# Retention and an ELU feed-forward on one core: two states moved to the end of the opening, four loads moved behind a transposition

## The chip, the cores and the metric

The kernel runs on one core of a Trainium2 chip. The metric is device microseconds of one execution. The engines go by the names of the profile: PE is TensorE, PEld its weight loads, DVE is VectorE, ACT is ScalarE, POOL is GpSimd, SP is SyncE, which only issues DMAs here.

## The reference

```python
scores = (1 / sqrt(64)) * q @ k.T                  # q, k, v: 8 batches, 8 heads, 576 rows, 64
D[h, i, j] = gamma[h] ** (i - j) if i >= j else 0  # gamma[h] = 1 - 2 ** (-5 - h)
x = (scores * D) @ v                               # heads side by side: 4608 x 512
h = x @ w_in                                       # 512 x 2048
g = where(h > 0, h, exp(min(h, 0)) - 1)
out = g @ w_out                                    # 2048 x 512, out 4608 x 512 float32
```

## The kernel before

**Retention.** The powers of gamma are split into a factor on the rows of q and one on the rows of k, so that a block of 128 rows needs its own masked scores and, for all that lies before it, one 64 x 64 state per head. A *unit* is one batch, one half of its first 512 rows (T is 0 or 1) and four of the eight heads; four units make a batch, numbered in order, so units 0 to 3 are batch 0 and unit 4 is the first of batch 1. The last 64 rows of four batches at a time make a *tail* (units 32 and 33). For a unit the kernel loads q, k and v (`ldq`, `ldk`, `ldv`, on SP), multiplies the four quarters of q and k by their factors (`cq0`, `cq1`, `ck0`, `ck1`, line 494), casts v (`cv`, line 545) and transposes q and k: units 0 to 6 on PE (`T`, line 558, copied out at line 564 by `cp`), unit 7 and all later ones with a DMA (`tr`, line 602). Units from number 8 on load q, k and v in two issues each (`ldq0_10`, `ldq1_10` and so on, line 412).

PE then computes scores (`sc`) and states; DVE masks the scores (`mask`, line 937); DVE, or ACT for the first, adds up the states (`mid`, `end`, lines 803 to 812). From the two sums come states with zeros beside the diagonal blocks, `bm` for the unit's own second half and `be` for whoever comes behind it (line 820, tile `s_end`; `bm` of units 0 and 1 is line 834). For a unit with T = 1, which is the case of units 2 and 3, nobody comes behind but the tail of the batch: `be2` and `be3` are read by unit 32 alone. The result goes through PSUM to `xt` (lines 972 to 993).

**Feed-forward.** Tokens are taken in blocks of 256 or 512. F1 multiplies `xt` by a column of w_in, ACT takes the exponential (`ex`, line 1145), ACT or DVE the maximum (`md`, lines 1153 and 1155), DVE joins them (`g`, line 1160), F2 multiplies g by w_out into the output. Weights come in eight pieces, `wi0` to `wi3` and `wo0` to `wo3`, issued by POOL (lines 471 and 479). F1 and F2 fill PE between the stretches of the units; a stretch (`S`) holds what the units before still need and the scores and states of the next.

**The order of the work.** Nothing of the order is written out by hand. Each step is an `Op` with a cost per engine that may do it, what it depends on, and a rank. `Plan.run` (line 68) goes through planned time and gives every free engine the ready step of the lowest rank (`pick`, line 99); a step with a choice of engines goes to the one that would end it first. The result is the order in which the instructions are issued, and each engine runs its own in that order. Three tables bear on the change: `ON` (line 212) binds a step to one engine, `RANKS` (line 202) adds to a rank, `HOLD` (line 201) makes POOL write one element into the tile of `ldq4` (`hold4`, line 431, rank -5), which keeps SP's loads from unit 4 on behind it. In a list `turn` stand steps that must have begun, not ended, before a step may. SP's loads form a chain by `turn`; a transposition has rank -1, loads have ranks from 9 up, so a transposition whose input is ready goes first.

```python
it.be = block(("end", n), ("s_end", it.b, it.T, it.w), f"be{n}", end)
return add(name, {"POOL": 0.62, "DVE": (0.42, 0.4 if it.early else 1.5)}, [dep], emit, it.rank + 3,
           take=[T(key[0], key, [P, 2, P], BF16)], use=[src])
...
held.append(add(f"hold{n}", {"POOL": 0.13}, [], emit_hold, -5, take=take))
...
it.turned.append(add(f"tr{n}", {"SP": 1.23}, list(it.cq.values()), emit, -1, ...
```

The ranks of units 2 and 3 are -56 and -52, so `be2` had rank -53 and `be3` -49; F1 and F2 start at rank 0. While the first 50 us of the plan have gaps on PE, small matmuls on zeros are put there.

Of the kernel before, what the change touches and what calls it, by code (L numbers as in the profile page):

```python
# [198 lines left out]

LEAD = 64  # L200
HOLD = {4: "wi0"}
RANKS = {}
TOGETHER = 1
EARLY = 5
LOOSE = True
# [3 lines left out]
POOL0 = 3.6  # L209
MERGE = {}  # L210
FROM = (8.96, 10.28, 13.13, 15.23, 17.0, 17.0, 17.44, 17.82)
ON = {'mid1': 'DVE', 'be2': 'DVE', 'md_1_0': 'ACT', 'xc1_2': 'DVE', 'cv0': 'DVE', 'md_1_1': 'ACT', 'cq12': 'DVE'}
DIRECT = True
PAIR = 8
FAR = 8
# [26 lines left out]
def kernel(  # L242
# [1069 lines left out]
    named = {op.name: op for op in plan.ops}  # L1312
# [6 lines left out]
    named["wo0"].turn.append(named["wi3"])  # L1319
    for name, e in ON.items():  # L1320
        if name in named and e in named[name].cost:
            named[name].cost = {e: named[name].cost[e]}
    for name, shift in RANKS.items():
        if name in named:
            named[name].rank += shift
# [64 lines left out]
```

## Time and profile before

| | |
|---|---|
| median of 3 runs | 298.99 us (298.35 to 299.23) |
| profiled execution | 299.29 us, span 297.6 us |
| PE busy | 291.7 us, 98% of the span, clock 1.00 |
| ACT, DVE, POOL busy | 66%, 60%, 46% |
| DMA queue of SP | 45.37 MB, 78.3% of 16 engines |
| DMA queue of POOL (weights) | 4.19 MB, 8.6% |
| chain that ended last | PE 86%, DMA 7%, POOL 3%, DVE 2% |

The span is what the profile covers from the first to the last instruction; the time of the execution is 1.69 us longer. Times in the text are microseconds from the span's start. A row of the timeline has its start, its length, the engine, the line and the operation, and behind them in brackets how long the engine stood idle before it and what ended that. A row of the chain of waits has start, length, and whose time it was; an engine's name with a q is its sequencer, which waits or issues.

### The profile page before, as it was taken

Reading aid. Unit: us, or ns where it says so; the run is one execution under the profiler, and the core shown is the slowest. Engines: PE = TensorE matmul, PEld = TensorE weight load, DVE = VectorE, ACT = ScalarE, POOL = GpSimd, SP = SyncE. Lnnn points to the kernel's source line nnn. Section 1 sums busy time; section 2 is a strip of 40 time slices with the busy share of each in tenths; the row PEclk is TensorE's granted clock in tenths of the full one; section 3 lists DMA queues with packets and bytes.
Section 4 is the critical chain, followed back from the end, with each engine's and each line's share of the span. In section 5 each row is a group of like instructions: output and inputs, shape, how many; then the busy total and the mean of one; then the engine's idle time right before and its main releaser. Section 6 shows DMA issues by size and latency. Waiting matters only on the chain.

```text
span 297.6 us, 8887 instructions
## 1 busy us (share of the span) xinstructions
PE 291.7 (98%) x3560; PEld 164.4 (55%) x3560; DVE 179.7 (60%) x323; ACT 195.1 (66%) x383; POOL 136.5 (46%) x257
## 2 busy tenths in 40 slices
PE   7999999999999999999999999999999999999996
PEld 3678746867776664545545454545444544444445
DVE  5999935838755849697756556666550169643300
ACT  2449823859768758778696868676772289777512
POOL 5880379956856755666534558542444000000000
PEclk9999999999999999999999999999999999999999
DMA  7999999999999999999999999996497410011132
GB/s 207 260 206 204 216 280 217 219 174 200 193 194 187 196 189 204 193 237 200 208 222 298 208 219 203 196 189 161 103 169 172 90 39 1 0 39 35 35 106 73
DMA packets 142010, 50.14 MB, mean 168 GB/s; under 512 B 120720, under 2 KB 137488, under 8 KB 141968
## 3 DMA queue, kind: packets, MB, share of 16 engines
q1 hardware_dynamic: 137744, 45.37, 78.3%
q0 software_dynamic: 4224, 4.19, 8.6%
q8 instruction: 28, 0.46, 0.7%
q14 instruction: 14, 0.11, 0.1%
HBM read 36.70 MB, written 9.44 MB: 155 GB/s over the span
## 4 chain that ended last, share of the span: by engine, by line
PE 86%; DMA 7%; POOL 3%; DVE 2%; SPq 1%; issue 0%; ACT 0%; ACTq 0%
PE f L276 84%; DMA rv<-in_v_dram 7%; PE sc L276 2%; POOL w_out_sb L479 1%; DVE pt L937 1%; SPq L422 1%; POOL w_in_sb L471 1%; POOL s_end L820 0%; POOL qkn L494 0%; DVE qkn L494 0%; PE f L558 0%; DVE s_end L820 0%; DVE s_mid L834 0%; POOL s_mid L820 0%; POOL vn L545 0%
## 5 line engine op out<-in xcount | busy, mean ns | idle before, releaser
L276 PE MATMUL f<-w_out_sb,g 128*128 128x512 bf16 (+2 forms) x608 | 141.1, 368 | 0.0
L276 PE MATMUL f<-xt,w_in_sb 128*128 128x256 bf16 (+1 forms) x768 | 138.2, 326 | 0.0
L1160 DVE SCALAR_TENSOR_TENSOR g<-e,f 128x512 bf16<-128x512 f32 x144 | 95.9, 684 | 69.0 <-ACT f L1153 53.2
L1145 ACT ACTIVATE e<-f 128x512 f32<-128x512 f32 x144 | 84.8, 597 | 33.7 <-PE f L276 25.7
L276 PEld LDWEIGHTS <-w_in_sb 128*128 128x128 bf16 x768 | 74.7, 98 | 53.5 <-DVE xt L988 0.4
L276 PEld LDWEIGHTS <-g 128*128 128x128 bf16 x608 | 56.6, 98 | 57.9
L1153 ACT ACTIVATE f<-f 128x512 f32<-128x512 f32 x116 | 68.5, 593 | 0.0
L494 POOL TENSOR_TENSOR qkn<-rqk,far_q 128x256 bf16<-128x256 f32 x48 | 28.9, 614 | 9.2 <-DMA rqk<-in_q_dram 9.0
L494 POOL TENSOR_TENSOR qkn<-rqk,far_k 128x256 bf16<-128x256 f32 x48 | 29.0, 616 | 7.6 <-DMA rqk<-in_k_dram 7.2
L1200 ACT COPY ot<-f 128x512 f32<-128x512 f32 (+2 forms) x30 | 16.8, 560 | 19.9 <-PE f L276 19.9
L545 POOL CAST vn<-rv 128x512 bf16<-128x512 f32 x28 | 17.1, 612 | 21.7 <-DMA rv<-in_v_dram 16.6
L972 ACT CAST xt<-f 128x512 bf16<-128x512 f32 x24 | 12.9, 589 | 16.1 <-PE f L276 16.1
L877 POOL CAST y<-mid 64x256 bf16<-64x256 f32 x36 | 14.3, 401 | 19.8 <-DVE mid L862 10.4
L1155 DVE TENSOR_SCALAR f<-f 128x512 f32<-128x512 f32 x28 | 19.4, 694 | 1.0 <-ACT e L1145 0.7
L931 DVE TENSOR_TENSOR pt<-sc,mask_t 128x1024 bf16<-128x1024 f32 x12 | 14.6, 1220 | 2.4 <-PE sc L276 2.4
L618 POOL TENSOR_TENSOR aside<-aside,gq 128x256 bf16<-128x256 f32 x16 | 9.4, 614 | 11.3 <-DMA aside<-in_k_dram 11.2
L494 POOL TENSOR_TENSOR qkn<-rqk,gq 128x256 bf16<-128x256 f32 x13 | 8.1, 633 | 12.3 <-DMA rqk<-in_q_dram 12.3
L877 ACT CAST y<-mid 64x256 bf16<-64x256 f32 x30 | 11.6, 402 | 2.1 <-DVE mid L860 1.0
L862 DVE TENSOR_TENSOR mid<-f,mid 128x256 f32<-128x256 f32 x24 | 10.2, 424 | 2.8 <-PE f L276 0.5
L276 PE MATMUL f<-pt,vn 64*64 64x64 bf16 (+1 forms) x512 | 11.5, 202 | 0.2 <-DVE pt L937 0.2
L993 ACT CAST xt<-f 128x256 bf16<-128x256 f32 x10 | 4.2, 452 | 10.8 <-PE f L276 10.8
L937 DVE TENSOR_TENSOR pt<-sc,mask 128x1024 bf16<-128x1024 f32 x8 | 9.8, 1220 | 2.2 <-PE sc L276 2.1
(92 smaller groups left out, 172.7 us busy)
## 6 DMA issues: line engine op xcount, KB each, us to landing
rqk<-in_q_dram SPq DMA_DIRECT2D x48, 128.0 KB, 3.9
rqk<-in_k_dram SPq DMA_DIRECT2D x48, 128.0 KB, 3.5
rv<-in_v_dram SPq DMA_DIRECT2D x48, 128.0 KB, 3.4
out_dram<-ot SPq DMA_DIRECT2D x18, 256.0 KB, 3.5
out_dram<-ot SPq DMA_DIRECT2D x19, 128.0 KB, 2.4
rqk<-in_q_dram SPq DMA_DIRECT2D x8, 256.0 KB, 6.8
rqk<-in_k_dram SPq DMA_DIRECT2D x8, 256.0 KB, 5.8
rv<-in_v_dram SPq DMA_DIRECT2D x8, 256.0 KB, 5.9
```

Of the source, the lines that this page charges most:

```text
L276: return pin(nc.tensor.matmul(*a, **kw))
L494: pin(alu[op.eng].tensor_tensor(dst, tiles[raw][:, :, e], g, ALU.mult))
L545: pin(copy[op.eng](tiles["vn", n], tiles["rv", n]))
L877: pin(copy[op.eng](dst, tiles[key][j * D : (j + 1) * D]))
L931: pin(nc.vector.tensor_tensor(tiles[it.pt].rearrange("p i h n -> p (i h n)")[:, : 2 * w * C].rearrange("p (i x n) -> p i x n", i=2, n=C), ...
L937: pin(nc.vector.tensor_tensor(tiles["pt", n].rearrange("p i h n -> p (i h) n"), tiles[it.sc].rearrange("p i (h n) -> p (i h) n", h=2), mas ...
L972: pin(copy[op.eng](by_block(it.xt)[:, 2 * it.T + c], tiles[xkey, c].rearrange("p (h n) -> p h n", n=P)))
L1145: pin(nc.scalar.activation(tiles[ekey], tiles[hkey], AF.Exp))
L1153: pin(nc.scalar.activation(ph, ph, AF.Relu))
L1155: pin(nc.vector.tensor_scalar_max(ph, ph, 0.0))
L1160: pin(nc.vector.scalar_tensor_tensor(tiles[gkey], tiles[ekey], -1.0, tiles[hkey], ALU.add, ALU.min))
L1200: pin(copy[op.eng](tiles[okey][:, :cols], tiles[pkey][:, :cols]))
```

## The change

`be2` is no longer bound to DVE, and the ranks of `be2` and `be3` rise by 60, to 7 and 11. `ldq0_10`, the first load of unit 10, may not begin before `tr7`, the DMA transposition of unit 7, has begun; by the chain, this holds for all later loads too.

```diff
-RANKS = {}
+AFTER = {"ldq0_10": "tr7"}
+RANKS = {"be2": 60, "be3": 60}
...
-ON = {'mid1': 'DVE', 'be2': 'DVE', 'md_1_0': 'ACT', 'xc1_2': 'DVE', 'cv0': 'DVE', 'md_1_1': 'ACT', 'cq12': 'DVE'}
+ON = {'mid1': 'DVE', 'md_1_0': 'ACT', 'xc1_2': 'DVE', 'cv0': 'DVE', 'md_1_1': 'ACT', 'cq12': 'DVE'}
...
+    for name, first in AFTER.items():
+        for one in (first if isinstance(first, tuple) else (first,)):
+            named[name].turn.append(named[one])
     for name, shift in RANKS.items():
         if name in named:
             named[name].rank += shift
```

## The prediction

> **What bounds the kernel now.** I read the page first: TensorE is busy for 291.7 us of a span of 297.6, no other engine above 66%, and the granted clock is full in every slice. So only TensorE's idle and waiting time can be won. The table by windows says where that is: 1.38 us idle before 5 us, 1.00 in 5 to 10, 0.27 and 0.11 in the next two, none from 20 to 35, 0.22 in 35 to 40, none again up to 100 us. The rest lies behind TensorE's last matmul (294.8 us). The list of TensorE's waits from 19 us to the end has one entry, 0.2 us, on a cast by POOL. The chain of waits tells what is behind that cast:
>
> ```profile
> 17.03 0.68 POOL qkn L494
> 17.71 3.00 POOL w_out_sb L479 x4
> 20.70 0.64 POOL s_end L820
> 21.35 0.05 POOL rqk L431
> 21.39 0.02 issue
> 21.41 0.37 SPq L422
> ...
> 22.37 15.56 DMA rv<-in_v_dram
> 37.94 0.05 issue
> 37.99 0.62 POOL vn L545
> ```
>
> The reader sees that POOL's block-diagonal state `be3` (0.64 us, line 820) stands directly ahead of the memset `hold4`, which lets SP ask for unit 4's q, k and v. They land at 30.64, 34.26 and 37.94, one every 3.65 us, because the weight pieces on the other DMA queue land between them (29.17, 32.79, 36.46, 40.15). TensorE's timeline shows what this costs:
>
> ```profile
> 35.26 0.60 PE L558 MATMUL f<-ident,qkn 128*128 128x128 bf16 x4
> 35.69 1.03 PE L276 MATMUL f<-w_out_sb,g 128*128 128x512 bf16 x4
> 36.65 0.42 PE L276 MATMUL sc<-qkT 64*64 64x128 bf16 x16
> 37.00 1.47 PE L276 MATMUL f<-w_out_sb,g 128*128 128x512 bf16 x6
> 38.65 0.32 PE L276 MATMUL f<-vn,qkn 64*64 64x64 bf16 x16 [0.18 <-POOL vn L545]
> ```
>
> Unit 4's key transposes take 0.43 us to the next row; the query ones, which waited for nothing, took 0.22 (31.99 to 32.22): 0.2 lost on k. The six matmuls from 37.00 last 1.65; six take 1.30 at 38.90, and each change to the small attention matmuls costs 0.09 anyway (the last one's step to them is 0.31 in 14 other places, not 0.22): 0.25 lost on v. Together **0.45 us** hangs on unit 4's loads.
>
> **The change, part by part.** I worked out the new order by hand from ranks and release rules; times are rows of the trace.
>
> *be3 behind hold4.* With rank 11 it loses to `hold4` (-5) when POOL is done with the weight issues at 20.70. The memset then starts 0.56 us sooner (21.25 to 20.69) and SP's first issue falls from 21.41 to 20.85. `be3` follows in a POOL idle until 30.77; only the tails (217 us) read it: cost nothing. Do the landings move as well? Unit 4's first packets show at 25.04, 3.6 us after the issue (about 1 us in the opening), so they stand in a line behind weight packets. All 16 engines finish ldq4 within 28.96 to 30.64, while a weight piece ends over 2.3 us (23.12 to 25.44): the start does not follow the ends of the pieces, so I take it to move with the issue. Bounds: 0.56 earlier, or not at all.
> The Trainium skill ("DMA: Bandwidth & Descriptors", Queues, rings and completion order) has each DMA engine take turns between queues, packet by packet. The trace agrees on the shares (from 27 us, 69 packets of one queue to 70 of the other in each half microsecond), but not on a start at once; with such a start, too, the landings would follow the issue.
>
> *be2 to the end, free to choose its engine.* Before, VectorE does it at 16.16 for 0.74 us:
>
> ```profile
> 15.03 1.22 DVE L937 TENSOR_TENSOR pt<-sc,mask 128x1024 bf16<-128x1024 f32 x1
> 16.16 0.74 DVE L820 TENSOR_TENSOR s_end<-end,diag 128x256 bf16<-128x256 f32 x1
> 16.83 0.41 DVE L494 TENSOR_TENSOR qkn<-rqk,gk 128x256 bf16<-128x256 f32 x1
> 17.16 0.41 DVE L564 COPY qkT<-f 128x512 bf16<-128x512 bf16 x1
> ```
>
> After, both halves of unit 3's scaled k (`ck03`, `ck13`) go to VectorE here, and `be2` takes `ck13`'s place on POOL (17.03, 0.68 us), ahead of the four w_out issues. VectorE: 2 x 0.41 in place of 0.74 + 0.41, or 0.74 + 0.41 if the first is slowed as `be2` was. So `ck13` is ready at 16.90 to 17.24 in place of 17.71, unit 3's second transposes end some 0.35 to 0.5 earlier, the copy behind them 0.25 to 0.5. But the state matmuls, done at 18.30 in that wait, now follow the scores (wait for `cv3`, ScalarE, 18.14), and `mid3` falls behind the mask on VectorE: 0.27 and 0.28 back. The first F1 matmul (18.91) moves by -0.15 to +0.14, the third group (21.50) by -0.2 to +0.1. I take **-0.1**. w_in piece 0 lands at 17.77 and piece 1 at 20.32, before both, and hide nothing.
> If `be2` on POOL overlaps `ck13`, one waits for the other; `be0` beside a POOL multiply took 0.83, alone 0.42. Then the w_out issues and `hold4` slip by up to 0.25, and of the 0.56 some 0.3 is left.
> The Trainium skill ("SBUF — State Buffer", Who interferes with whom) speaks against this part: VectorE with two SBUF inputs and GpSimd lock each other out for a whole instruction. The trace agrees where two multiplies meet (0.91 at 10.71), and shows no slowing beside a DMA issue (0.42 at 14.50). By the rule alone `hold4` would always slip, and the sum would be some 0.3.
>
> *Sum up to 39 us.* Without its two waits and with the opening's 0.1, TensorE would come to unit 4's state matmuls at 38.65 - 0.45 - 0.1 = 38.10. The cast of v ends at 38.60 - 0.56 = 38.04 at best, 38.3 if `hold4` slips. So **0.3 to 0.55, I take 0.5**. Next in line is w_out piece 3: it gives up a third of 0.56 us of DMA and lands near 40.35; its first matmul moves from 41.19 to about 40.7. Covered by 0.3.
>
> *Loads of unit 10 behind tr7.* SP's order, before:
>
> ```profile
> 51.08 1.01 SPq L412 DMA_DIRECT2D rv<-in_v_dram  x2
> 52.18 1.01 SPq L412 DMA_DIRECT2D rqk<-in_q_dram  x2
> 53.28 1.00 SPq L412 DMA_DIRECT2D rqk<-in_k_dram  x2
> 54.38 1.35 SPq L602 DMA_TRANSPOSE qkT<-qkn  x1
> ```
>
> The four issues of unit 10's q and k now follow the transposition. Its input is complete when POOL's last multiply of unit 7 ends, 51.89; SP gets there at 52.18: no new wait, nothing idles behind it. tr7 lands 3.44 us after its issue (57.82), so near 55.6. The four loads land about 1.4 to 2 us later (55.02 becomes near 57); POOL takes the first at 57.53: covered by 0.5. Units 10 and 11 meet TensorE at 74, with their last transposition landed at 71.59. TensorE waits for nothing from 40 to 100 us, so an earlier tr7 wins nothing itself. It lets unit 7's stretch go ahead of one F2 and one or two F1 groups (58.35 to about 56.6). With TensorE 0.5 sooner its scores come at 56.4, tr7 0.8 ahead of them, as much as now (58.66 against 57.82). **0.** Without this part the margin would be 0.3. From there to the end TensorE does the same matmuls, and behind the last one (294.8) the stores are the same.
>
> Profiled execution: 299.29 us (span 297.6 and 1.69 around it), minus 0.5: 298.8. It stands 0.3 above the median, so the forecast for the median is 298.99 - 0.5 = **298.5**, a gain of 0.17%. A difference within 0.3% (0.9 us) is about what a measurement of this kernel can tell from no change; the three runs spread over 0.88.
>
> **Rivals.** *Nothing gained* (0.10; 299.0): the loads wait for a moment that the issue does not set. For: 3.6 us from issue to first packet. Against: the even start over the engines. Then v lands at 37.94 again and TensorE meets the same wait, whatever the opening gave.
> *More than the gate allows* (0.20; 298.0): an earlier issue gets into the line ahead of a whole weight piece, the loads land 2 us or more sooner, the cap at 38.04 falls; 0.45, the opening's 0.2, and up to 0.3 from a new order around units 7 to 9 with fewer changes between large and small matmuls (each 0.09 going in, 0.1 coming out). Against: w_out piece 3 then lands 1.2 us later, at 41.35, and stops TensorE near 40.5.
> *Slower* (0.24; 300.2): unit 7's stretch stands earlier in TensorE's fixed order, and its transposition does not keep up. The transpositions of this size took 3.3 to 5.9 us from issue to landing in this trace. At 5.9, tr7 lands at 58.1, TensorE stands 1.7 us at 56.4, and with the 0.5 gained before the loss is 1.2. From a landing 1.4 us past 56.4 on (57.8), the whole change loses over 0.9. Against: the same backlog, three or four loads, lies ahead of tr7 in both orders, and it took 3.44 behind it.
>
> **Numbers.** Forecast 0.46, of which 0.05 ends beyond 0.9 us by the spread of the runs; rivals 0.10, 0.20, 0.24. Faster by over 0.3%: 0.20 + 0.05 = 0.25; within: 0.41 + 0.10 = 0.51; slower: 0.24. The forecast's own range is 298.1 to 298.8; the range for 8 in 10 takes in the third case and the slower one up to 1.4 us: 297.8 to 300.4.
>
> **What would show it.** SP's first issue for unit 4 at 20.85 to 21.1; ldv4 landing at 37.4 to 37.7; the two waits at 35.3 and 38.5 gone; state matmuls of unit 4 at 38.1 to 38.35; tr7 issued near 52 and landed before its scores; TensorE's last matmul near 294.3. A wait of TensorE at unit 7, or v at 37.9 again, would make the forecast wrong.

## The result, and the profile after

The changed kernel took 299.46 us (median of 16 runs, 298.35 to 301.17) where the kernel before, on the same chip, took 298.69 (16 runs, 298.19 to 299.43). The ratio is 1.0026, with a 95% interval of 1.0015 to 1.0037: it became 0.78 us slower. The profiled execution took 300.17 us, its span 298.4.

From the page of the changed kernel, TensorE's busy time and its granted clock in 40 slices:

```profile
PE 292.6 (98%) x3557; PEld 165.4 (55%) x3557; DVE 181.4 (61%) x325; ACT 194.8 (65%) x383; POOL 135.0 (45%) x255
...
PEclk9799999999999999999999999999999999999999
```

TensorE is still what bounds the kernel. In the second slice the clock was granted at 0.7 in the mean, half speed from 7.63 to 11.05 us. The program is the same up to there, and three of 35 runs of the kernel before, beside the first experiments, have the same mean clock (0.993 to 0.994). So this is taken for chance. It puts the whole opening of this one profile back by 0.9 us (first F1 matmul 19.81 in place of 18.91), and times from it are therefore compared as distances. It doesn't explain the loss: without the three of its 16 runs at this clock, the changed kernel's median is still 299.39.

VectorE in the changed kernel (start, length, engine, line, operation), and then POOL:

```profile
15.96 1.22 DVE L938 TENSOR_TENSOR pt<-sc,mask 128x1024 bf16<-128x1024 f32 x1
17.10 1.07 DVE L495 TENSOR_TENSOR qkn<-rqk,gk 128x256 bf16<-128x256 f32 x2
18.09 0.41 DVE L565 COPY qkT<-f 128x512 bf16<-128x512 bf16 x1
```

```profile
17.96 0.68 POOL L821 TENSOR_TENSOR s_end<-end,diag 128x256 bf16<-128x256 f32 x1
18.59 3.04 POOL L480 DMA_DIRECT2D w_out_sb<-in_moe_w_out_dram  x4
21.59 0.15 POOL L432 MEMSET rqk<- 128x1 f32 x1
21.65 0.66 POOL L821 TENSOR_TENSOR s_end<-end,diag 128x256 bf16<-128x256 f32 x1
...
37.81 0.61 POOL L546 CAST vn<-rv 128x512 bf16<-128x512 f32 x1 [2.40 <-DMA rv<-in_v_dram]
```

The order is the one that the prediction derived: both halves of unit 3's scaled k on VectorE, one of them stretched by `be2` beside it on POOL (1.07 for the two), `be2` ahead of the w_out issues, `hold4` directly behind them, `be3` last. (The changed kernel has one more line, so its line numbers are one higher.) TensorE from 36 us:

```profile
36.22 0.39 PE L559 MATMUL f<-ident,qkn 128*128 128x128 bf16 x4
36.44 1.03 PE L277 MATMUL f<-w_out_sb,g 128*128 128x512 bf16 x4
37.40 0.42 PE L277 MATMUL sc<-qkT 64*64 64x128 bf16 x16
37.75 1.47 PE L277 MATMUL f<-w_out_sb,g 128*128 128x512 bf16 x6
39.15 0.32 PE L277 MATMUL f<-vn,qkn 64*64 64x64 bf16 x16
```

Both waits are gone: the transposes of k go over to the next row after 0.22 us (0.43 before), the six matmuls after 1.40 (1.65 before). Unit 4's state matmuls come 0.50 us later than in the profile of before, in an opening that was 0.90 later: 0.4 was won here against that one profile. SyncE and TensorE around unit 7:

```profile
50.66 2.04 SPq L413 DMA_DIRECT2D rv<-in_v_dram  x2
52.80 1.35 SPq L603 DMA_TRANSPOSE qkT<-qkn  x1
54.21 1.18 SPq L413 DMA_DIRECT2D rqk<-in_q_dram  x2
55.43 1.06 SPq L413 DMA_DIRECT2D rqk<-in_k_dram  x2
```

```profile
58.08 0.28 PE L277 MATMUL f<-qkT,s_mid 128*128 128x128 bf16 x2
58.29 0.42 PE L277 MATMUL sc<-qkT 64*64 64x128 bf16 x16
```

The transposition of unit 7 landed at 56.17, 3.4 us after its issue, and 2.1 ahead of its scores; nothing waits. So the signs that the prediction asked for are there as far as unit 7, and the kernel is slower all the same. Two sizes differ: unit 7's stretch moved forward by 0.9 us against the scores of unit 5 (12.60 us behind them in place of 13.46), where the prediction has 1.75, and TensorE's last matmul comes only 0.3 us sooner behind the first F1 matmul, where it has 0.5.

### The profile page after: what moved, and what is told of

Read it like the earlier page. It is cut to its first block, busy times and chain, and to the rows that moved or that the text cites. A ratio compares the mean times of both kernels' runs of the same rounds, so it can differ in the third digit from the quotient of the medians.

```text
span 298.4 us, 8879 instructions
## 1 busy us (share of the span) xinstructions
PE 292.6 (98%) x3557; PEld 165.4 (55%) x3557; DVE 181.4 (61%) x325; ACT 194.8 (65%) x383; POOL 135.0 (45%) x255
## 4 chain that ended last, share of the span: by engine, by line
PE 94%; DVE 3%; DMA 2%; SPq 0%; issue 0%; ACT 0%; ACTq 0%
PE f L277 90%; PE sc L277 2%; DMA rv<-in_v_dram 2%; PE f L1353 1%; DVE pt L938 1%; PE f L559 1%; DVE qkT L565 0%; DVE qkn L495 0%; SPq L423 0%; DVE xt L994 0%; DVE end L813 0%; DVE vn L546 0%; DVE s_mid L835 0%; ACT ot L1201 0%; DVE mid L804 0%
## 5 line engine op out<-in xcount | busy, mean ns | idle before, releaser
L1154 ACT ACTIVATE f<-f 128x512 f32<-128x512 f32 x114 | 67.5, 593 | 0.0
L878 POOL CAST y<-mid 64x256 bf16<-64x256 f32 x33 | 12.7, 395 | 21.0 <-ACT ot L1201 8.4
L1156 DVE TENSOR_SCALAR f<-f 128x512 f32<-128x512 f32 x30 | 20.6, 693 | 2.0 <-ACT e L1146 1.8
L878 ACT CAST y<-mid 64x256 bf16<-64x256 f32 x33 | 12.8, 401 | 1.7 <-DVE mid L863 0.8
```

The lines of the kernel that those rows point to most:

```text
L878: pin(copy[op.eng](dst, tiles[key][j * D : (j + 1) * D]))
L1154: pin(nc.scalar.activation(ph, ph, AF.Relu))
L1156: pin(nc.vector.tensor_scalar_max(ph, ph, 0.0))
```

## The experiments

All ratios are to the kernel before on the same chip, with 95% intervals. Two numbers are read from each profile beside them, in the table at the end of this section: the time from the first F1 matmul to the scores of unit 5 (the part of the opening in which the loads of unit 4 and w_out arrive), and from there to the end of the span.

### The two parts, and the smallest edit

```diff
states_only:  AFTER = {}            (be2 and be3 moved, no load moved)
loads_only:   RANKS = {}, 'be2': 'DVE' back in ON
be3_only:     AFTER = {}, RANKS = {"be3": 60}, 'be2': 'DVE' back in ON
after_again:  the changed kernel once more
```

> Only the states of units 2 and 3 are moved (ranks, and be2 free to choose); the loads of unit 10 stand as before. The issue order from about 40 us on is that of the kernel before. Theory S (the redrawn order behind 52 us costs): TensorE's two waits for unit 4 go, 0.3 to 0.5 us faster than before. Theory O (the opening costs: both halves of ck3 on VectorE, scores ahead of states, mid3 behind the mask): 0.5 to 0.8 us slower than before. Theory L (the earlier loads push the weight pieces back, and that costs): also slower, 0.3 to 0.8.

> Only the loads of unit 10 wait for tr7; be2 and be3 stand as before, so the opening is that of the kernel before, and from tr7 on the order is that of the changed kernel. Theory S: 0.5 to 1.1 us slower than before, with a wait of TensorE in some stretch behind 52 us that the kernel before does not have. Theories O and L: no difference (within 0.2 us), no new wait.

> Only be3 is moved, behind hold4: a swap of two POOL instructions, every other engine's order is that of the kernel before. Theories S and O: unit 4's loads go out 0.56 us sooner, both waits at 35 and 38 us shrink, 0.3 to 0.5 us faster than before. Theory L: the w_out pieces land about 0.2 us or more later, no gain or up to 0.5 us slower.

> The changed kernel once more, for a second profile of it. In its first profile TensorE's granted clock was 0.5 from 7.6 to 11.0 us, in a part of the program that the change does not touch, and the first F1 matmul came 0.9 us later than before. If that is chance, a profile at full clock has the first F1 matmul at 18.8 to 19.0 and the whole is 0.4 to 0.8 slower than before all the same (theories S, O, L); if that drop belongs to the change, it is there again.

Measured: states alone 1.0003 (0.9987 to 1.0019), loads alone 1.0009 (0.9989 to 1.003), `be3` alone 1.0007 (0.9992 to 1.0022), the changed kernel again 1.0023 (1.0005 to 1.0041). The loss is repeated, and neither part alone shows it beyond its interval. But neither shows the gain either: with `hold4` 0.6 us sooner in its place, and no wait for unit 4 in the profile, the states part is not faster. The second profile of the changed kernel has a new wait: its first F1 matmul came early, at 18.33, and TensorE then lost 0.6 us before 40.82 to the fourth piece of w_out. By its middle value the states part (0.1 us slower) meets none of the three theories, and its interval, from 0.4 us faster to 0.6 slower, touches all of them.

### Lighter loads, and the loads' place alone

```diff
before_light, after_light (line 411, shortened):
+ if n >= 10: dma_start(tile, src[it.b, 4*it.w + 2*it.T + e, :4*P, :])  # as many bytes, other rows, in pieces of 1 KB
swap_on_sp:       before's order, the four loads of unit 10 put behind tr7
swap_back_on_sp:  loads_only's order, the four loads put ahead of tr7
```

> The kernel before, in which the loads of units 10 to 31 take other rows of the same batch, as many bytes in pieces of 1 KB in place of 256 B, so that the DMA engines have less to do behind 50 us; retention of these units is computed on wrong rows. The order of every engine is that of the kernel before. Theory D (in the changed kernel the transpositions of units 12 to 19 land too close to their stretches: in its two profiles 0.3 to 1.3 us ahead, before 1.4 to 2.9): this kernel gains little, 0 to 0.4 us against before. Theory P (the redrawn order itself costs on TensorE, wherever the data are): the same.

> The changed kernel with the same lighter loads of units 10 to 31 (the same part computed on wrong rows). Theory D: with the transpositions early again, what the opening wins is kept, 0.3 to 0.6 us faster than before_light. Theory P: 0.4 to 0.9 us slower than before_light, as the changed kernel is against the kernel before.

> The kernel before with one edit to the finished order: the four loads of q and k of unit 10 are issued behind tr7 instead of ahead of it; every other engine, and SP everywhere else, is as before. Theory D: the loads' delay is enough, 0.2 to 0.5 us slower than before. Theory P: no difference, within 0.2 us.

> The kernel with only the loads moved (states as before), in whose finished order the four loads are put back ahead of tr7; TensorE, VectorE, ScalarE and POOL keep the order that the move gave them, with unit 7's stretch earlier. Theory D: unit 7's scores wait for tr7 (some 1 to 1.5 us of TensorE at 57 us), which is lost again. Theory P: 0.3 to 0.5 us slower from the order alone, and the wait at unit 7 on top of it.

Measured: before_light 1.0000 (0.9988 to 1.0012), after_light 1.0022 (1.0002 to 1.0043), swap_on_sp 1.0017 (0.9994 to 1.004), swap_back_on_sp 1.0026 (1.0012 to 1.0041). In the table by windows the DMA share fell from 1.27 and 1.29 (before, 120 to 130 and 130 to 140 us) to 0.79 and 0.71 (before_light), and the time did not move (the share counts each of the packets under way at once, so it can pass 1); the changed kernel stayed slower with the same relief. So theory D, that the loads press on later transpositions, does not explain the loss. Theory P, the order that the planner redraws, agrees with swap_back_on_sp, which has that order without the moved loads; the eleven runs of swap_on_sp spread from 298.55 to 301.09, and it was measured again below. In swap_back_on_sp unit 7's stretch stands earlier while its transposition does not:

```profile
59.60 0.42 PE L277 MATMUL sc<-qkT 64*64 64x128 bf16 x16 [0.24 <-DMA qkT<-qkn]
```

That is the wait of the prediction's slower rival: a stretch moved forward, and its transposition not. It is 0.24 us, and the changed kernel does not have it. This one profile also stood 0.36 us for w_in's second piece and lost 1.2 to w_out's fourth, so its span says little of the order.

### Nobody waits for the fourth piece of w_out

```diff
before_w3free, states_w3free, after_w3free (shortened):
- mm(pm, g[...], w_out_sb[:, ft, n0:n1], ...)
+ mm(pm, g[...], w_out_sb[:, ft - 4 if blk in (0, 1) and ft > 11 else ft, n0:n1], ...)
states_swap: states_only's order, the four loads of unit 10 put behind tr7
```

> The kernel before; in the first two token blocks F2 reads the rows of w_out's third piece in place of its fourth (its output of these blocks is not the reference's). The fourth piece is still loaded, at the same place in the queue, but TensorE no longer waits for it near 40 us. Theory W (the fourth piece of w_out is the next bound in the opening, and in many executions it, not v of unit 4, sets when TensorE goes on): 0 to 0.3 us faster than the kernel before, since that one meets this wait in some executions only (0.7 in one profile, none in another). Rival R (the opening's end is set elsewhere): no change.

> The states part alone (ranks of be2 and be3, be2 free), with the same edit of F2 in the first two blocks (output of these not the reference's). Theory W: now unit 4's loads come earlier and nobody waits for the fourth piece, so the gain that the prediction asked for appears: 0.4 to 0.6 us faster than the kernel before, 0.3 or more faster than the kernel before with the same edit. Rival R (the gain is lost elsewhere, as with be2 on GpSimd, or is lost in noise): as without the edit, 0.0 to 0.2 slower than the kernel before.

> The changed kernel with the same edit of F2 in the first two blocks (output of these not the reference's). Theory W, with the loads part's own +0.4 on top: 0.0 to 0.2 us faster than the kernel before, where the changed kernel is 0.7 slower. If the loads part's loss too lies at the fourth piece: 0.4 or more faster. Rival R: 0.7 slower as without the edit.

> The states part alone with its own order of the other four engines, and in the finished order the four loads of q and k of unit 10 moved right behind the transposition of unit 7: the whole change, but without the order that the planner redraws after it. Theory P (the redrawn order of TensorE and the others behind 52 us costs the 0.4): as the states part alone, +0.0 to +0.2 us against the kernel before. Theory L (the later loads themselves cost): +0.5 to +0.8, as the changed kernel.

Measured: before_w3free 0.9994 (0.998 to 1.0008), states_w3free 1.0009 (0.9991 to 1.0028), after_w3free 1.0006 (0.9984 to 1.0028) and, for states_swap, 1.0012 (0.9995 to 1.0028). With nobody waiting for the piece, the kernel before was most likely 0.2 us faster, and the states part was not: its ratio is 0.0015 above that of the kernel before with the same edit (medians 299.10 and 298.44), where theory W expects 0.3 us or more of gain. The piece does stop TensorE in some executions, but it is not what keeps the states part from gaining. Theory W in its strong form falls. states_swap lies between what theories P and L expect and decides nothing.

### The kernel before again, and the last store

```diff
before_again: the kernel before, unchanged
before_store, states_store, after_store (line 1208, shortened):
- nc.sync.dma_start(out[...], ...)
+ (nc.scalar if n0 and n1 == DM else nc.sync).dma_start(out[...], ...)     # the very last store only
```

> The kernel before, built a second time with the changed kernel's line numbers, nothing else. What it measures against the kernel before is the uncertainty of all other comparisons: 0.0 within 0.15 us in the mean. If it comes out 0.2 slower, as the states part and be3 alone did, these two cost nothing. Its profile is a second look at the opening of before: theory M (unit 4's loads land at the edge, and the two waits that the prediction counts on are there in few executions) expects no wait of 0.4 for v, or one for w_out's fourth piece in its place; the prediction's own reading expects 0.45 again.

> The kernel before, but the very last store (128 x 128) is issued by ScalarE behind its own copy instead of by SyncE. In the profiles SyncE's issue of the store before it took 0.33 to 1.11 us, and where it took over 0.55 the last store was late by up to 0.36. Theory E (this delay is larger in the kernels with the states moved, 0.18 to 0.36 in six profiles of eight, and none in six profiles of six without): 0.0 to 0.1 faster than the kernel before. Rival N (the delay strikes by chance, all kernels alike): 0.1 to 0.2 faster, like the two others of this edit.

> The states part alone, with the last store issued by ScalarE. Theory E: the 0.2 to 0.3 us of the states part lie here, so 0.0 against the kernel before, and no more than 0.1 slower than the kernel before with the same edit. Rival N: 0.2 slower than the kernel before with the same edit.

> The changed kernel, with the last store issued by ScalarE. Theory E: of the 0.7 us, 0.25 goes, so 0.4 to 0.5 slower than the kernel before; what is left belongs to the loads part. Rival N: 0.7 slower than the kernel before with the same edit.

Measured: before_again 1.0009 (0.9994 to 1.0023), before_store 1.0011 (0.9994 to 1.0027), states_store 1.0013 (0.9997 to 1.0029), after_store 1.0025 (1.0008 to 1.0041). The kernel against itself gives 1.0009: that much is nothing. The kernels with one part alone cannot be told from it, but for swap_back_on_sp, which has a wait of its own making at unit 7. The whole change stands above it, at 1.0026, 1.0023, 1.0025, and 1.0022 with light loads. Where nobody waits for w_out's last piece it is at 1.0006, 0.0012 above the kernel before with the same edit; that interval is too wide to tell. Theory E finds no support: with the last store off SyncE the changed kernel is as much slower as with it. The interval takes in the theory's 0.4 to 0.5 us too, so it is not ruled out; and no kernel of this edit came out faster, as rival N had it for the kernel before.

The second profile of the kernel before answers the larger question. POOL and TensorE in before_again:

```profile
37.32 0.61 POOL L546 CAST vn<-rv 128x512 bf16<-128x512 f32 x1 [2.45 <-DMA rv<-in_v_dram]
```

```profile
36.74 1.47 PE L277 MATMUL f<-w_out_sb,g 128*128 128x512 bf16 x6
38.14 0.32 PE L277 MATMUL f<-vn,qkn 64*64 64x64 bf16 x16
...
40.25 0.60 PE L277 MATMUL f<-w_out_sb,g 128*128 128x512 bf16 x2
41.53 1.89 PE L277 MATMUL f<-w_out_sb,g 128*128 128x512 bf16 x8 [0.68 <-DMA w_out_sb<-in_moe_w_out_dram]
```

The same program as before, the first F1 matmul at 18.86 as against 18.91, and no wait for v: six matmuls in 1.40, the cast done at 37.93, 0.21 ahead of the state matmuls. TensorE stops at w_out's fourth piece instead. In states_store the opening had no wait at all (unit 5's scores at 44.62), and TensorE met two others later, in its timeline:

```profile
96.31 0.32 PE L277 MATMUL sc<-qkT 64*64 64x64 bf16 x16 [0.41 <-DMA qkT<-qkn]
...
147.20 0.32 PE L277 MATMUL sc<-qkT 64*64 64x64 bf16 x16 [0.29 <-DMA qkT<-qkn]
```

### The loads' place alone, and the loads part, a second time

> A second measurement, beside the next kernel: the kernel before with its own order on four engines, and only the four loads of unit 10 moved behind the transposition of unit 7 on SyncE. Theory P (the order that the planner redraws behind it costs): 0.0 to 0.2 us slower than the kernel before, and 0.3 or more faster than the loads part alone. Theory L (the later loads cost): 0.4 or more slower than the kernel before, as the loads part alone.

> A second measurement of the loads part alone, with the planner's redrawn order. Both theories: 0.4 us slower than the kernel before, as the first time; at 0.1 or less the loads part would cost nothing and the loss of the changed kernel would need the states part. From the scores of unit 5 to the end of the span the profiles so far have 252.7 us for the old order and 252.9 for the redrawn one; theory P expects 252.9 here and 252.7 in the run beside it.

Measured on one chip: 0.9999 (0.9975 to 1.0023) and 0.9999 (0.9979 to 1.0019); by medians 298.93 and 299.19 against 298.91. Neither the moved loads nor the redrawn order costs an amount that this can show alone; the 0.4 us that the expectation counted on from the first time is not there again, though intervals of 0.6 to 0.7 us to each side do not exclude it. swap_on_again is also the opening of before in an execution where nothing stops TensorE:

```profile
38.55 0.32 PE L277 MATMUL f<-vn,qkn 64*64 64x64 bf16 x16
...
40.66 2.33 PE L277 MATMUL f<-w_out_sb,g 128*128 128x512 bf16 x10
```

### All profiles together

Opening "old" is that of before; "be" has the states moved. The wait is what TensorE lost between 35 and 43 us, measured against the same rows where nothing waits; the idle time that a row shows in brackets can be up to 0.2 shorter.

| kernel | opening | first F1 | hold4 to ldv4 landed | wait | unit 5's scores | from there to the end |
|---|---|---|---|---|---|---|
| before | old | 18.91 | 16.69 | 0.45, k and v | 45.20 | 252.4 |
| before_again | old | 18.86 | 16.08 | 0.8, w_out | 45.52 | 252.8 |
| before_light | old | 18.55 | 16.11 | 0.9, w_out | 45.23 | 252.8 |
| before_store | old | 18.54 | 16.13 | 0.3, w_out | 44.65 | 252.8 |
| before_w3free | old | 18.24 | 16.18 | none, w_out can't | 44.05 | 252.3 |
| swap_on_sp | old | 19.86 | 16.18 | none | 45.68 | 252.3 |
| swap_on_again | old | 19.28 | 16.18 | none | 45.10 | 252.5 |
| loads_only | old | 19.60 | 16.07 | none | 45.41 | 252.7 |
| loads_again | old | 19.80 | 15.59 | none | 45.62 | 252.8 |
| swap_back_on_sp | old | 19.27 | 16.09 | 1.2, w_out | 46.70 | 252.6 |
| be3_only | be3 alone | 18.86 | 16.22 | none | 44.68 | 253.1 |
| states_only | be | 18.74 | 16.18 | none | 44.62 | 252.3 |
| states_w3free | be | 18.22 | 16.22 | none, w_out can't | 44.10 | 252.7 |
| states_swap | be | 18.38 | 16.38 | none | 44.26 | 252.7 |
| states_store | be | 18.75 | 16.12 | none | 44.62 | 253.5 |
| after | be | 19.81 | 16.16 | none | 45.69 | 252.8 |
| after_again | be | 18.33 | 16.17 | 0.6, w_out | 44.81 | 252.8 |
| after_light | be | 18.19 | 16.25 | 0.15, w_out | 44.22 | 253.2 |
| after_w3free | be | 18.86 | 16.27 | none, w_out can't | 44.74 | 253.1 |
| after_store | be | 18.26 | 16.19 | 0.7, w_out | 44.87 | 253.3 |

Three things are seen in it. The landing of ldv4 follows `hold4` by 15.6 to 16.4 us in 19 profiles of 20; the one with 16.69 is the profile that the prediction was made from. Without a wait, the old opening takes 25.82 us from the first F1 matmul to unit 5's scores (45.10 - 19.28 in swap_on_again), the one with both states moved 25.88 (44.62 - 18.74). And what follows grows with the change: 252.6 in the mean of the seven profiles of before's own order, 252.7 with the loads part (three), 252.9 with one or both states moved (five), 253.0 with both parts (five). That is 0.5 us between the first and the last, while the profiles within a group spread over 0.2 to 1.2.

## Why the prediction was wrong

Two steps failed: the 0.45 us that was counted as gained on unit 4's loads, and that nothing was counted as lost from unit 7 to the end.

**The bound** was read rightly: TensorE, and only its waits.

**"Together 0.45 us hangs on unit 4's loads"** is the step of the gain that failed. The rows said so for one execution, and there it was true: its ldv4 landed 0.5 us later behind `hold4` than in any other profile of that opening. In the nine others the cast of v ended ahead of its need, by 0.1 to 0.2 us in seven (37.93 for 38.14, 38.46 for 38.55, 38.66 for 38.87) and by 0.7 in two, and no wait for it was seen in any. One in ten, times 0.45, is worth some 0.05 us. It was chance that the one profile at hand had this wait. The first F1 matmul, the loads and the weight pieces each come a little by chance, and a wait of 0.45 us is shorter than what they move by; the prediction's sum took one execution's meeting of the three for the kernel's. In all nine profiles with both states moved the cast ended 0.5 to 0.8 us ahead, but there was hardly a wait to win.

**The loads move with the issue**: right, and exactly so. `hold4` came 0.60 us sooner behind unit 2's scores (6.15 in place of 6.75), as the order on POOL said, and ldv4 kept its 16.1 to 16.2 us behind it. The rival that nothing moves, and the one that a whole weight piece is overtaken, are both ruled out by that.

**"Covered by 0.3"**, of w_out piece 3, was mis-sized. In the profiles it landed anywhere from 39.0 to 42.7 us and stopped TensorE in four of the nine openings of before in which it could (0.3 to 1.2 us) and in three of seven with both states moved. It is not next in line behind v: in the kernel before it already stops TensorE more often than v does. The edit that frees TensorE from it shows its price in before: 0.2 us by the ratio, 0.36 by the medians (298.44 as against 298.80), with an interval that reaches past zero.

**be2, "I take -0.1"**: it is +0.03. From unit 2's scores to the third group of F1 it took 7.00 us in before, before_again and before_w3free, and 7.03 in states_w3free, states_swap and after_w3free (21.03 - 14.00). The two engines' slowing of each other came as the bounds had it (1.07 for two multiplies on VectorE beside `be2` on POOL, in place of 2 x 0.41). It was VectorE that waited: `be2` on POOL took 0.68 us, as long as the multiply in its place before. So `hold4` did not slip, and of the prediction's two bounds for this 0.56 held and 0.3 did not.

**The loads of unit 10, "0"**: near enough to what could be measured. tr7 kept 3.4 us from issue to landing, no wait came at unit 7, and the part alone measured 1.0009 and 0.9999. Only the stretch's own move was half of what was forecast (0.9 us for 1.75). The slower rival, a transposition that lands 1.7 us too late there, did not happen.

**"From there to the end TensorE does the same matmuls, and behind the last one (294.8) the stores are the same"** is the other step that failed: it put nothing behind unit 7, and the loss that the profiles show lies behind the opening. With no gain in the opening, the forecast's own sum would have been zero. In the means of the profiles, about 0.5 of the 0.78 us shows behind unit 5's scores.

Some 0.2 of it lies at the very end. From the start of TensorE's last matmul to the end of the span it is 3.08 us in the mean of the ten profiles with the old opening (3.04 to 3.15), and 3.29 in the five with both parts (3.11 to 3.40). SyncE's issue of the last store but one took 0.45 to 0.85 us in those ten and 0.80 to 1.17 in these five, and the very last store then started late: by 0.1 to 0.3 us in six of the eight profiles with a state moved and every store on SyncE, by less than 0.1 in all nine of the old opening. Why moving a state near 20 us should do that is open, and it isn't shown that the runs lose these 0.2: the changed kernel with that store on ScalarE is no faster by its ratio.

The other 0.3 lies before TensorE's last matmul. Part of it is seen: waits of 0.24 to 0.41 for a DMA transposition in five profiles of twenty (at 60, 66, 96, 122 and 147 us), in the old order too (0.25 at 66 us in before_store), and in one of the five with both parts. The shortest time that any profile took for each stretch between two scores adds up to 252.05 us in the old order and 252.18 in the redrawn one, 0.13 more without any wait. Whether the redrawn order leaves the transpositions less room can't be told: that of unit 15 landed 2.65 us ahead of its scores in before and 0.32 in after, but 1.11 ahead in before_again and 1.31 in after_again.

The rest isn't located, and the split is a rough one: the spans of those seven and five profiles differ by 0.3 us in the mean (297.6 and 297.9), where the runs say 0.7 to 0.8. The middle values of the parts alone (1.0003 and 1.0013 for the states, 1.0009 and 0.9999 for the loads) add up to less than the loss, but their intervals take it in, so whether the two parts only add up or act on each other is open. No kernel that does the whole computation has a ratio below 0.9999.

## What to carry to other kernels

Before a wait of a few tenths is counted as a gain, look at it in a second profile of the same kernel, or ask by how much its transfer lands apart from one execution to the next; a wait shorter than that is worth its size times how often it comes. Where several transfers land within a microsecond of their need, removing one wait makes the next one count, so the sum goes by the margin of all of them. And run the kernel against itself: here that gave 1.0009, as much as either half of the change.

## What the runs showed of the hardware that was not expected

The time from `hold4`, SyncE's go-ahead, to the landing of the third load, through a queue that shares its engines with the weights, was 16.1 to 16.3 us in 17 profiles of 20. The last weight piece beside it landed anywhere from 17.4 to 21.1 us behind the same memset.

In before_w3free, weight pieces land 2.5 to 2.6 us apart before unit 4's loads come (17.24, 19.78, 22.38, 25.01) and 3.6 to 3.7 beside the loads (28.62, 32.31, 35.92, 39.65). The Trainium skill ("DMA: Bandwidth & Descriptors", Queues, rings and completion order) has the queues take turns packet by packet; the slower pace beside the loads agrees with that.

SyncE's issue of the last store but one took 0.45 to 1.17 us in 19 profiles of 20, where the two issues before it took 0.33. In six profiles, all with a state moved, it held the very last store up by 0.1 to 0.3. SyncE's last four issues in before, and then in the changed kernel, from the start of the first to the end of the last:

```profile
291.83 3.62 SPq L1208 DMA_DIRECT2D out_dram<-ot  x4
```

```profile
292.41 3.91 SPq L1209 DMA_DIRECT2D out_dram<-ot  x4
```

Giving the very last store to ScalarE did not make any of the three kernels faster, so what makes the issue long stays open.

Loads in 1 KB pieces took two fifths off the DMA share in the middle of the kernel (1.28 to 0.75 from 120 to 140 us) and changed the time by 0.0% (1.0000, 0.9988 to 1.0012): the busy queue was no bound there.
